# Masks added on TensorE in PSUM, batch 2's value means summed by accumulating transfers, weight splits moved off GpSimd

## Chip, cores and metric

One of the eight cores of one Trainium2 chip runs the kernel. The metric is the device time of one execution in microseconds (us); lower is better.

## What is computed

Batch 2, 8 heads, 768 tokens, head size 64, all in float32. Attention sees, for every query, the keys less than 16 positions away and 24 summaries, one for each block of 32 keys: the block's maximum of k and its mean of v. Then come two feed-forward layers over all 1536 tokens.

```python
k_sum = k.reshape(B, H, nb, 32, D).max(axis=3)
v_sum = v.reshape(B, H, nb, 32, D).mean(axis=3)
scores_l = where(|i - j| < 16, scale * q @ k.T, -1e9)
scores_s = scale * q @ k_sum.T + log(32)
a = softmax(concat([scores_l, scores_s]))
x = a @ concat([v, v_sum])
x = square(relu(x @ w_in)) @ w_out
xn = rms_norm(x) * rms_g
out = (silu(xn @ w_gate) * (xn @ w_val)) @ w_out2
```

## The kernel before

**Attention.** The 12 groups of 128 queries (6 for each batch) are worked off one after another. `scores(g)` makes two PSUM tiles of 128 x 4 x 120 scores: for each tile of 64 queries 96 keys around it and the 24 block maxima (L411). `softmax(g)` lets VectorE add a mask tile to them into SBUF (L444: -1e9 outside the window, log 32 on the summaries), takes the maxima (L448), and ScalarE takes eight exponentials with their sums (L450). `ptrans(g)` transposes the result on TensorE, and `av(g)` multiplies it with `vx`, which has four slots of 120 rows: 96 rows of v from the DMA (`vload`, L407) and 24 rows of block means. The means come from `vmean(b, c)` (L370): three loads of v (`vm_load`, L353), six float32 matmuls against the averaging matrix `ind`, and a ScalarE copy from PSUM (L387 to two slots of `vx`, L388 to `vm`); `vmput` lets GpSimd copy `vm` to the other slots (L394).

**Weights.** They arrive as 64-bit floats. `Units` takes them through a chain, one unit of 128 x 512 at a time: load (`load64`), two ScalarE instructions (`conv_a`, L176 and L177), four on VectorE (`conv_b`, L183 to L190), and `split` (L193) into a high part, rounded to the type that TensorE multiplies fastest (fp32r), and the rest. The first eight units (`wi` 0 to 3 and `wo` 0 to 3) are split on GpSimd (L197, L200), all later ones by a ScalarE cast and a VectorE subtraction.

**Feed-forward.** Every product is three fp32r matmuls, high by high, high by low and low by high (L512, L533). The first four `wi` and `wo` units run pair by pair of groups between the attention steps (`h_pair`, `y_pair`, from L699 on); the rest follows in two long loops (from L760 on).

**What sets the order.** Every engine and every DMA queue works off its own list in order. The lists are made by a planner that runs the program through a model of the chip: an instruction goes to its engine's list as soon as the model has it ready, and among those that are ready the one traced first goes first. `after(m)` puts an edge from the marked instruction to what its block traces, and only to instructions on the marked instruction's own engine; it orders issue and makes nothing wait for an end. PSUM tiles come in turn from pools of two buffers each (`psA`, tags "a" and "x" from L629 on). SyncE issues all transfers of this kernel.

Of the kernel before, what the change touches and what calls it, by code (L numbers as in the profile page):

```python
# [32 lines left out]
def tile_window_attention_moe_moe2(  # L33
# [13 lines left out]
    nc = tc.nc  # L47
# [29 lines left out]
    scale = 1.0 / math.sqrt(D)  # L77

    cpool = ctx.enter_context(tc.tile_pool(name="cpool", bufs=1))
    wpool = ctx.enter_context(tc.tile_pool(name="wpool", bufs=1))  # L80
    xpool = ctx.enter_context(tc.tile_pool(name="xpool", bufs=NCH))
    hpool = ctx.enter_context(tc.tile_pool(name="hpool", bufs=2))
# [5 lines left out]
    ident = cpool.tile([P, P], F32, name="ident")  # L88
    make_identity(nc, ident)
    um = cpool.tile([P, KW + QT], F32, name="um")  # L90
    masks = {}
    ind = cpool.tile([P, NB + P // (BLK // 2) * (NC2 - 1)], F32, name="ind")
    ss = cpool.tile([P, NG], F32, name="ss")
    rinv = cpool.tile([P, NG], F32, name="rinv")

    def constants():
        n = ind.shape[1]
        o = P // (BLK // 2) * (NC2 - 1)
        pb = BLK // 2
        nc.gpsimd.memset(ind, 1.0 / BLK)  # L100
        nc.gpsimd.affine_select(
            out=ind, in_=ind, compare_op=ALU.is_ge, fill=0.0, base=pb * o,
            pattern=[[-pb, n]], channel_multiplier=1,
        )
        nc.gpsimd.affine_select(
            out=ind, in_=ind, compare_op=ALU.is_ge, fill=0.0, base=pb - 1 - pb * o,
            pattern=[[pb, n]], channel_multiplier=-1,
        )
        nc.gpsimd.memset(um, 0.0)
        nc.gpsimd.affine_select(  # L110
            out=um, in_=um, compare_op=ALU.is_ge, fill=NEG, base=-1,
            pattern=[[1, KW + QT]], channel_multiplier=-1,
        )
        nc.gpsimd.affine_select(
            out=um, in_=um, compare_op=ALU.is_ge, fill=NEG, base=2 * WIN - 1,
            pattern=[[-1, KW + QT]], channel_multiplier=1,
        )


        mid = cpool.tile([P, NK], F32, name="mask_mid")  # L120
        nc.gpsimd.memset(mid, math.log(BLK))
        for j, n, o in ((0, G0, 0), (K1, QT, G0)):
            nc.gpsimd.tensor_copy(mid[0:QT, j : j + n], um[0:QT, o : o + n])
            nc.gpsimd.tensor_copy(mid[QT:P, j : j + n], um[QT:P, QT + o : QT + o + n])
        first = cpool.tile([P, NK], F32, name="mask_first")
        nc.gpsimd.tensor_copy(first, mid)
        nc.gpsimd.memset(first[0:QT, 0:WIN], NEG)
        last = cpool.tile([P, NK], F32, name="mask_last")
        nc.gpsimd.tensor_copy(last, mid)
        nc.gpsimd.memset(last[QT:P, NK - WIN : NK], NEG)  # L130
        masks.update(first=first, mid=mid, last=last)

# [55 lines left out]
        nc.vector.tensor_tensor(xi, xi, r, op=ALU.add)  # L190
        return x

    def split(x, nm, pool):  # L193
        w_ = wslot(f"w_{nm}")
        hi, lo = w_[:, 0], w_[:, 1]
        if pool:
            nc.gpsimd.tensor_copy(hi, x)  # L197
        else:
            nc.scalar.copy(hi, x)
        (nc.gpsimd if pool else nc.vector).tensor_tensor(lo, x, hi.bitcast(F32), op=ALU.subtract)  # L200
        return hi, lo

    class Units:
# [9 lines left out]
        def tick(self):  # L213
            n, units = self.n, self.units
            if n[3] < n[2]:
                u = units[n[3]]
                W[u] = split(self.x.pop(u), "%s%d" % u, n[3] < 2 * ROUNDS1[0])
                n[3] += 1
            if n[2] < n[1]:
                u = units[n[2]]  # L220
                with after(*((("mx", 0),) if n[2] == 0 else ())):
                    self.x[u] = conv_b(*self.a.pop(u))
                n[2] += 1
            if n[1] < n[0]:
                u = units[n[1]]
                self.a[u] = conv_a(self.raw.pop(u), "%s%d" % u)
                n[1] += 1
            self.load(min(n[2] + self.ahead, len(units), self.used + self.cap))
# [117 lines left out]
    def prep_kend(b, eng, w0, w1):  # L346
# [3 lines left out]
            state[b].unsqueeze(2).to_broadcast([P, NPAIR, w1 - w0, NB]),  # L350
        )

    def vm_load(b, c):  # L353
        state[("v", b, c)] = raw_chunk(v, b, c, f"vr{b}_{c}")

# [14 lines left out]
    def vmean(b, c):  # L370

        if c == 0:
            state["vmps"] = psA(f"vmean{b}", [K1, DM])
        ps = state["vmps"][G0:K1]
        pb = BLK // 2
        nb2 = P // pb
        vr = state.pop(("v", b, c))
        for e in range(2):
            nc.tensor.matmul(  # L379
                ps, ind[:, nb2 * (NC2 - 1 - c) : nb2 * (NC2 - 1 - c) + NB], vr[:, :, e, :],  # L380
                start=(c == 0 and e == 0), stop=(c == NC2 - 1 and e == 1),
            )
        if c == NC2 - 1:
            vm = ap_.tile([K1, DM], F32, tag="vm", name=f"vm{b}", bufs=1)[G0:K1]
            state["vm"] = vm
            if b == 0:
                nc.scalar.copy(vrows(0, 2), ps.unsqueeze(1).to_broadcast([NB, 2, DM]))  # L387
            nc.scalar.copy(vm, ps)  # L388

    def vrows(i0, n):  # L390
# [20 lines left out]
    def scores(g):  # L411
        b, r = divmod(g, GPB)
        qT = state[("qT", g)][:, :, (r % 2) * P : (r % 2 + 1) * P]
        sl = [psA(f"s{e}_{g}", [P, NPAIR, NK]) for e in range(2)]
        for p in range(NPAIR):
            for x in range(2):
                for e in range(2):
# [4 lines left out]
                        sl[e][QT * u : QT * u + QT, p, :],  # L422
                        qT[rr, p, QT * u : QT * u + QT],
                        kT[rr, p, o : o + NK],
                        start=True, stop=True,
                    )
        state[("s", g)] = sl

    def softmax(g):
# [10 lines left out]
        for i in range(parts):  # L440
            hs = slice(n * i, n * i + n)
            tv, m_, s_ = t[:, hs], mx[:, hs], sm[:, hs]
            for e in range(2 // parts * i, 2 // parts * (i + 1)):
                nc.vector.tensor_tensor(  # L444
                    te[:, e], sl[e], mk.unsqueeze(1).to_broadcast([P, NPAIR, NK]), op=ALU.add
                )
            if EXPACT(g):
                mark[("mx", g)] = nc.vector.reduce_max(m_, tv, axis=AX.X, negate=True)  # L448
                for h in range(hs.start, hs.stop):
                    mark[("exp", g)] = nc.scalar.activation(  # L450
                        t[:, h], t[:, h], AF.Exp, bias=mx[:, h : h + 1], accum_out=sm[:, h : h + 1]
                    )
            else:
                nc.vector.reduce_max(m_, tv, axis=AX.X)
# [148 lines left out]
        prep_load(0, c)  # L603
    qload(0)
    units1.load(1)
    for c in range(NC2):
        vm_load(0, c)
    vload(0)
    vload(1)
    qload(2)  # L610
    for j in (0, LK - WIN):
        nc.gpsimd.memset(kT[:, :, j : j + WIN], 0.0)
    nc.gpsimd.memset(vx[0:WIN, 0], 0.0)
# [7 lines left out]
    scores(0)  # L621
    softmax(0)
    scores(1)
    for c in range(NC2):
        vmean(0, c)
    vmput(2, 2)
    units1.load(8)
    softmax(1)
    rot["tags"] = ("a", "x")  # L629
    qprep(2)  # L630
    ptrans(0)
    group(2)
    av(0)
    vload(2)
    ptrans(1)
# [63 lines left out]
    for k_ in range(NK2):  # L699
# [10 lines left out]
        if not last:  # L710
            av(g)
        if g == GPB - 1:
            for c in range(NC2):
                vmean(1, c)
            vmput(0, 2)
        if g + 2 < NG:
            group(g + 2)
            if k_ == 0:
                for c in range(NC2):
                    prep_load(1, c)  # L720
            if g + 2 == GPB + 1:
                vmput(2, 2)
        y_pair(k_, 0)
# [2 lines left out]
        if k_ == 0:  # L726
# [1 line left out]
            prep_k(1, 0)  # L728
            y_pair(k_, 2, (lambda: prep_k(1, 1), lambda: prep_k(1, 2)))
            prep_kend(1, nc.gpsimd, 0, NW1)  # L730
            for c in range(NC2):
                vm_load(1, c)
        else:
            if g + 3 < NG:
                qprep(g + 3)
# [125 lines left out]
```

## Time and profile before

| | us |
|---|---|
| median of 3 runs | 668.17 (667.84 to 668.64) |
| the profiled execution's own time | 667.06 |
| its span, first to last instruction | 665.4 |

All rows below come from the one profiled execution. Its busy shares: TensorE 96%, VectorE 61%, ScalarE 46%, GpSimd 4%. A group's row gives the line, the engine, the operation, the tile written and those read, the shapes and the count, then the busy time in us and the mean of one in ns, then the engine's idle time just before. L12 is line 12 of the kernel printed above; SPq is SyncE's transfer queue; PEld is the load of a stationary operand, which runs beside other matmuls.

### The profile page before, as it was taken

The numbers are of one execution on the slowest core, as the hardware profiler recorded it, in microseconds if no ns is written. First come the engines' busy times: TensorE is split into PE (matmuls) and PEld (weight loads), VectorE is DVE, ScalarE is ACT, GpSimd is POOL, SyncE is SP. The second block draws the span as 40 slices with busy tenths as digits, with TensorE's granted clock in tenths as the row PEclk, the third lists the DMA queues.
The fourth block names the chain that finished last, engine by engine and source line by source line (L and its number), as shares of the span: only waits on it lengthen the run. The fifth ranks groups of instructions, "written<-read, shape, count | busy, mean of one in ns | idle before, by whom it ended". The sixth has DMA issues, their size and how long they took to land.

```text
span 665.4 us, 9357 instructions
## 1 busy us (share of the span) xinstructions
PE 642.0 (96%) x3644; PEld 530.8 (80%) x3644; DVE 402.9 (61%) x716; ACT 304.6 (46%) x656; POOL 27.3 (4%) x45
## 2 busy tenths in 40 slices
PE   7768997999999999999999999999999999999997
PEld 6566976888888888888888888888888888888885
DVE  4798777759999389528484894299613271313132
ACT  4875666557675266227253773267411231111110
POOL 3153110000000000000000000000000000000000
PEclk9878998999999999999999999999999999999999
DMA  9994644215412313101131351025300000001011
GB/s 241 290 222 112 152 136 142 75 39 179 138 64 95 96 64 96 32 1 64 32 96 32 97 162 60 1 60 161 97 0 1 0 1 0 1 1 63 1 64 64
DMA packets 76957, 53.70 MB, mean 81 GB/s; under 512 B 45040, under 2 KB 71664, under 8 KB 76912
## 3 DMA queue, kind: packets, MB, share of 16 engines
q1 hardware_dynamic: 76912, 53.09, 27.0%
q8 instruction: 29, 0.48, 0.3%
q14 instruction: 16, 0.13, 0.1%
HBM read 49.94 MB, written 3.15 MB: 80 GB/s over the span
## 4 chain that ended last, share of the span: by engine, by line
PE 87%; DVE 5%; SPq 3%; ACT 2%; issue 1%; DMA 1%; DVEq 0%; ACTq 0%
PE y L533 19%; PE h L512 18%; PE v L512 15%; PE g L512 15%; PE z L533 15%; ACT t L450 2%; PE xps L491 2%; PE pps L470 1%; SPq L308 1%; PE s L421 1%; SPq L407 1%; PE vmean L379 1%; PE xps L503 1%; PE qps L366 1%; DMA qr<-in_q_dram 1%
## 5 line engine op out<-in xcount | busy, mean ns | idle before, releaser
L512 PE MATMUL h<-xhi,w_wi 128*128 128x512 f32 (+1 forms) x480 | 134.2, 352 | 1.3 <-ACT xhi L481 1.3
L533 PE MATMUL y<-w_wo,hhi 128*128 128x512 f32 x384 | 119.0, 394 | 0.1
L807 DVE TENSOR_TENSOR sg<-v,sg 128x512 f32<-128x512 f32 x36 | 24.9, 691 | 131.2 <-PE v L512 131.2
L512 PEld LDWEIGHTS h<-xhi,w_wi 128*128 128x128 f32 x480 | 86.3, 192 | 13.3 <-ACT xhi L481 1.5
L512 PE MATMUL v<-xhi,w_wv 128*128 128x512 f32 x288 | 94.8, 390 | 0.0
L512 PE MATMUL g<-xhi,w_wg 128*128 128x512 f32 x288 | 94.5, 390 | 0.0
L533 PE MATMUL z<-w_wp,hhiz 128*128 128x512 f32 x288 | 88.0, 389 | 0.0
L512 PE MATMUL h<-xlo,w_wi 128*128 128x512 f32 (+1 forms) x240 | 84.4, 352 | 3.0 <-DVE xlo L482 3.0
L533 PEld LDWEIGHTS y<-w_wo,hhi 128*128 128x128 f32 x384 | 71.5, 189 | 14.8 <-ACT hhi L523 0.4
L533 PE MATMUL y<-w_wo,hlo 128*128 128x512 f32 x192 | 74.2, 394 | 0.2 <-DVE hlo L524 0.2
L805 ACT ACTIVATE sg<-g 128x512 f32<-128x512 f32 x36 | 21.5, 597 | 102.1 <-PE g L512 99.9
L512 PEld LDWEIGHTS v<-xhi,w_wv 128*128 128x128 f32 x288 | 54.1, 188 | 11.2
L512 PEld LDWEIGHTS g<-xhi,w_wg 128*128 128x128 f32 x288 | 54.0, 188 | 11.2
L533 PEld LDWEIGHTS z<-w_wp,hhiz 128*128 128x128 f32 x288 | 54.0, 188 | 11.1
L660 ACT ACTIVATE r<-h 128x512 f32<-128x512 f32 x48 | 28.6, 596 | 67.5 <-PE h L512 67.4
L512 PE MATMUL v<-xlo,w_wv 128*128 128x512 f32 x144 | 56.1, 389 | 0.0
L512 PE MATMUL g<-xlo,w_wg 128*128 128x512 f32 x144 | 56.0, 389 | 0.0
L533 PE MATMUL z<-w_wp,hloz 128*128 128x512 f32 x144 | 55.4, 389 | 0.0
L523 ACT CAST hhiz<-sg 128x512 fp32r<-128x512 f32 x36 | 22.3, 620 | 68.6 <-DVE sg L807 68.3
L512 PEld LDWEIGHTS h<-xlo,w_wi 128*128 128x128 f32 x240 | 46.2, 192 | 8.8 <-DVE xlo L482 3.2
L661 DVE TENSOR_TENSOR r<-h,r 128x512 f32<-128x512 f32 x48 | 32.9, 685 | 32.4 <-ACT r L660 32.4
L533 PEld LDWEIGHTS y<-w_wo,hlo 128*128 128x128 f32 x192 | 36.0, 189 | 8.1 <-DVE hlo L524 0.6
(133 smaller groups left out, 918.7 us busy)
## 6 DMA issues: line engine op xcount, KB each, us to landing
raw_wi<-in_moe_w_in_dram SPq DMA_DIRECT2D x16, 512.0 KB, 4.9
raw_wo<-in_moe_w_out_dram SPq DMA_DIRECT2D x16, 512.0 KB, 4.3
raw_wg<-in_moe_w_gate_dram SPq DMA_DIRECT2D x12, 512.0 KB, 3.5
raw_wv<-in_moe_w_val_dram SPq DMA_DIRECT2D x12, 512.0 KB, 3.6
raw_wp<-in_moe_w_out_dram SPq DMA_DIRECT2D x12, 512.0 KB, 3.5
kr<-in_k_dram SPq DMA_DIRECT2D x12, 256.0 KB, 4.2
qr<-in_q_dram SPq DMA_DIRECT2D x12, 256.0 KB, 3.9
vr<-in_v_dram SPq DMA_DIRECT2D x6, 512.0 KB, 4.9
```

Source lines behind the costliest of these rows:

```text
L308: nc.sync.dma_start(t[:, j].rearrange("p (h d) -> p h d", h=H), src[b, :, o : o + P, :].rearrange("h p d -> p h d"),)
L366: nc.tensor.transpose(ps[:, p, :], qr[:, j, p * P : (p + 1) * P], ident)
L379: nc.tensor.matmul(ps, ind[:, nb2 * (NC2 - 1 - c) : nb2 * (NC2 - 1 - c) + NB], vr[:, :, e, :], start=(c == 0 and e == 0), stop=(c == NC2 - ...
L450: mark[("exp", g)] = nc.scalar.activation(t[:, h], t[:, h], AF.Exp, bias=mx[:, h : h + 1], accum_out=sm[:, h : h + 1])
L491: nc.tensor.matmul(ps[QT * e : QT * e + QT, o : o + QT], vx[:, (2 * g + u) % NVX, 2 * p + e, :], pT[:, e * NPAIR + p, QT * u : QT * u + QT ...
L512: nc.tensor.matmul(ps, a_, b_, start=(i == 0), stop=(i == tot - 1))
L523: nc.scalar.copy(hi[:, 0:n], s[:, 0:n])
L533: nc.tensor.matmul(y, a_[:, ms], b_, start=(first and i == 0), stop=(last and i == 2))
L660: nc.scalar.activation(t, ps, AF.Relu)
L661: nc.vector.tensor_tensor(t, ps, t, op=ALU.mult)
L805: nc.scalar.activation(t, psg, AF.Silu)
L807: nc.vector.tensor_tensor(t, psv, t, op=ALU.mult)
```

## The change

Groups 0 to 3 get their masks on TensorE: ahead of a score tile's matmuls, one fp32r matmul of the identity with the mask's rounded part, and behind them one with the mask's rest, all accumulating in PSUM. The maxima and exponentials then read PSUM. `split` runs on ScalarE and VectorE for all units. The queries of groups 2 and 3 and a second weight unit are loaded ahead of v, and the means of batch 1 are queued behind the scores of group 2; one of their two copies goes from ScalarE to VectorE. For batch 2, the three loads of v and six matmuls become eight transfers issued from GpSimd, 96 x 512 floats each, of which the last seven add into the first one's tile, and a single matmul over 96 partitions.

```diff
@@ -77,6 +77,7 @@
     scale = 1.0 / math.sqrt(D)
 
     cpool = ctx.enter_context(tc.tile_pool(name="cpool", bufs=1))
+    cpool.tile([P, 0], F32, name="left")
     wpool = ctx.enter_context(tc.tile_pool(name="wpool", bufs=1))
     xpool = ctx.enter_context(tc.tile_pool(name="xpool", bufs=NCH))
     hpool = ctx.enter_context(tc.tile_pool(name="hpool", bufs=2))
@@ -88,8 +89,16 @@
     ident = cpool.tile([P, P], F32, name="ident")
     make_identity(nc, ident)
     um = cpool.tile([P, KW + QT], F32, name="um")
-    masks = {}
+    masks, mhi = {}, {}
+    NPE = 4
+    identr = cpool.tile([P, P], F32R, name="identr")
+    mlo = cpool.tile([P, NK], F32R, name="mlo")
+    for nm in ("first", "mid"):
+        mhi[nm] = cpool.tile([P, NK], F32R, name=f"mhi_{nm}")
     ind = cpool.tile([P, NB + P // (BLK // 2) * (NC2 - 1)], F32, name="ind")
+    NE = 8
+    PV = S // NE
+    indv = cpool.tile([PV, NB], F32, name="indv")
     ss = cpool.tile([P, NG], F32, name="ss")
     rinv = cpool.tile([P, NG], F32, name="rinv")
 
@@ -105,6 +114,16 @@
         nc.gpsimd.affine_select(
             out=ind, in_=ind, compare_op=ALU.is_ge, fill=0.0, base=pb - 1 - pb * o,
             pattern=[[pb, n]], channel_multiplier=-1,
+        )
+        pv = BLK // NE
+        nc.gpsimd.memset(indv, 1.0 / BLK)
...
         nc.gpsimd.memset(um, 0.0)
         nc.gpsimd.affine_select(
@@ -129,6 +148,12 @@
         nc.gpsimd.tensor_copy(last, mid)
         nc.gpsimd.memset(last[QT:P, NK - WIN : NK], NEG)
         masks.update(first=first, mid=mid, last=last)
+        nc.gpsimd.tensor_copy(identr, ident)
+        nc.gpsimd.tensor_copy(mhi["first"], first)
+        nc.gpsimd.tensor_copy(mhi["mid"], mid)
+        nc.gpsimd.tensor_tensor(
+            mlo, mid, mhi["mid"].bitcast(F32), op=ALU.subtract
+        )
 
 
 
@@ -190,14 +215,11 @@
         nc.vector.tensor_tensor(xi, xi, r, op=ALU.add)
         return x
 
-    def split(x, nm, pool):
+    def split(x, nm):
         w_ = wslot(f"w_{nm}")
         hi, lo = w_[:, 0], w_[:, 1]
-        if pool:
-            nc.gpsimd.tensor_copy(hi, x)
-        else:
-            nc.scalar.copy(hi, x)
-        (nc.gpsimd if pool else nc.vector).tensor_tensor(lo, x, hi.bitcast(F32), op=ALU.subtract)
+        nc.scalar.copy(hi, x)
+        nc.vector.tensor_tensor(lo, x, hi.bitcast(F32), op=ALU.subtract)
         return hi, lo
 
     class Units:
@@ -214,7 +236,7 @@
             n, units = self.n, self.units
             if n[3] < n[2]:
                 u = units[n[3]]
-                W[u] = split(self.x.pop(u), "%s%d" % u, n[3] < 2 * ROUNDS1[0])
+                W[u] = split(self.x.pop(u), "%s%d" % u)
                 n[3] += 1
             if n[2] < n[1]:
                 u = units[n[2]]
@@ -350,6 +372,22 @@
             state[b].unsqueeze(2).to_broadcast([P, NPAIR, w1 - w0, NB]),
         )
 
+    vsum = xpool.tile([P, KD, CH], F32R, tag="xhi", name="vsum")
+    vsum = vsum[0:PV, 0].bitcast(F32).rearrange("p (h d) -> p h d", h=H)
+
+    def vs_load(b):
+        src = v[b].rearrange("h (p e) d -> p h e d", e=NE)
+        nc.gpsimd.dma_start(vsum, src[:, :, 0, :])
+        for e in range(1, NE):
+            nc.gpsimd.dma_start(vsum, src[:, :, e, :], accum_op=ALU.add)
+
+    def vs_mean(b):
+        ps = psA(f"vmean{b}", [K1, DM])[G0:K1]
+        nc.tensor.matmul(ps, indv, vsum.rearrange("p h d -> p (h d)"), start=True, stop=True)
+        vm = ap_.tile([K1, DM], F32, tag="vm", name=f"vm{b}", bufs=1)[G0:K1]
+        state["vm"] = vm
+        nc.scalar.copy(vm, ps)
+
     def vm_load(b, c):
         state[("v", b, c)] = raw_chunk(v, b, c, f"vr{b}_{c}")
 
@@ -384,7 +422,7 @@
             vm = ap_.tile([K1, DM], F32, tag="vm", name=f"vm{b}", bufs=1)[G0:K1]
             state["vm"] = vm
             if b == 0:
-                nc.scalar.copy(vrows(0, 2), ps.unsqueeze(1).to_broadcast([NB, 2, DM]))
+                nc.vector.tensor_copy(vrows(0, 2), ps.unsqueeze(1).to_broadcast([NB, 2, DM]))
             nc.scalar.copy(vm, ps)
 
     def vrows(i0, n):
@@ -412,6 +450,11 @@
         b, r = divmod(g, GPB)
         qT = state[("qT", g)][:, :, (r % 2) * P : (r % 2 + 1) * P]
         sl = [psA(f"s{e}_{g}", [P, NPAIR, NK]) for e in range(2)]
+        wide = [P, NPAIR, NK]
+        if g < NPE:
+            for s_ in sl:
+                mh = mhi["mid" if r else "first"]
+                nc.tensor.matmul(s_, identr, mh.unsqueeze(1).to_broadcast(wide), start=True, stop=False)
         for p in range(NPAIR):
             for x in range(2):
                 for e in range(2):
@@ -422,8 +465,13 @@
                         sl[e][QT * u : QT * u + QT, p, :],
                         qT[rr, p, QT * u : QT * u + QT],
                         kT[rr, p, o : o + NK],
-                        start=True, stop=True,
+                        start=g >= NPE, stop=g >= NPE,
                     )
+        if g < NPE:
+            for s_ in sl:
+                mark[("s", g)] = nc.tensor.matmul(
+                    s_, identr, mlo.unsqueeze(1).to_broadcast(wide), start=False, stop=True
+                )
         state[("s", g)] = sl
 
     def softmax(g):
@@ -440,15 +488,23 @@
         for i in range(parts):
             hs = slice(n * i, n * i + n)
             tv, m_, s_ = t[:, hs], mx[:, hs], sm[:, hs]
-            for e in range(2 // parts * i, 2 // parts * (i + 1)):
+            for e in range(2 // parts * i, 2 // parts * (i + 1)) if g >= NPE else ():
                 nc.vector.tensor_tensor(
                     te[:, e], sl[e], mk.unsqueeze(1).to_broadcast([P, NPAIR, NK]), op=ALU.add
                 )
             if EXPACT(g):
-                mark[("mx", g)] = nc.vector.reduce_max(m_, tv, axis=AX.X, negate=True)
+                src = [t[:, h] for h in range(H)]
+                if g < NPE:
+                    src = [s_[:, p] for s_ in sl for p in range(NPAIR)]
+                    for e in range(2 // parts * i, 2 // parts * (i + 1)):
+                        mark[("mx", g)] = nc.vector.reduce_max(
+                            mx[:, NPAIR * e : NPAIR * (e + 1)], sl[e], axis=AX.X, negate=True
+                        )
+                else:
+                    mark[("mx", g)] = nc.vector.reduce_max(m_, tv, axis=AX.X, negate=True)
                 for h in range(hs.start, hs.stop):
                     mark[("exp", g)] = nc.scalar.activation(
-                        t[:, h], t[:, h], AF.Exp, bias=mx[:, h : h + 1], accum_out=sm[:, h : h + 1]
+                        t[:, h], src[h], AF.Exp, bias=mx[:, h : h + 1], accum_out=sm[:, h : h + 1]
                     )
             else:
                 nc.vector.reduce_max(m_, tv, axis=AX.X)
@@ -603,11 +659,12 @@
         prep_load(0, c)
     qload(0)
     units1.load(1)
+    qload(2)
+    units1.load(2)
     for c in range(NC2):
         vm_load(0, c)
     vload(0)
     vload(1)
-    qload(2)
     for j in (0, LK - WIN):
         nc.gpsimd.memset(kT[:, :, j : j + WIN], 0.0)
     nc.gpsimd.memset(vx[0:WIN, 0], 0.0)
@@ -621,15 +678,16 @@
     scores(0)
     softmax(0)
     scores(1)
-    for c in range(NC2):
-        vmean(0, c)
-    vmput(2, 2)
+    softmax(1)
     units1.load(8)
-    softmax(1)
+    qprep(2)
     rot["tags"] = ("a", "x")
-    qprep(2)
     ptrans(0)
     group(2)
+    with after(("s", 2)):
+        for c in range(NC2):
+            vmean(0, c)
+    vmput(2, 2)
     av(0)
     vload(2)
     ptrans(1)
@@ -710,14 +768,15 @@
         if not last:
             av(g)
         if g == GPB - 1:
-            for c in range(NC2):
-                vmean(1, c)
+            vs_mean(1)
             vmput(0, 2)
         if g + 2 < NG:
             group(g + 2)
             if k_ == 0:
                 for c in range(NC2):
                     prep_load(1, c)
+                with after(("s", 4)):
+                    vs_load(1)
             if g + 2 == GPB + 1:
                 vmput(2, 2)
         y_pair(k_, 0)
@@ -728,8 +787,6 @@
             prep_k(1, 0)
             y_pair(k_, 2, (lambda: prep_k(1, 1), lambda: prep_k(1, 2)))
             prep_kend(1, nc.gpsimd, 0, NW1)
-            for c in range(NC2):
-                vm_load(1, c)
         else:
             if g + 3 < NG:
                 qprep(g + 3)
```

## Rows read from the trace of the kernel before

**Rows 1.** The page's head: the span and TensorE's busy time.

```profile
span 665.4 us, 9357 instructions
...
PE 642.0 (96%) x3644; PEld 530.8 (80%) x3644; DVE 402.9 (61%) x716; ACT 304.6 (46%) x656; POOL 27.3 (4%) x45
```

**Rows 2.** Busy time by engine in stretches: length, busy us (instructions), granted clock, DMA.

```profile
12.00:28.48 16.48, 12.26 (x113) 6.94 (x111) 10.85 (x25) 12.54 (x44) 3.54 (x4) 0.90 0.96 266
28.48:57.21 28.73, 20.60 (x261) 18.00 (x262) 28.73 (x49) 20.76 (x59) 12.17 (x11) 0.88 0.86 233
...
89.24:112.66 23.42, 19.52 (x219) 16.91 (x219) 18.01 (x34) 20.86 (x70) 2.02 (x2) 1.00 0.51 158
```

**Rows 3.** Chain that ended last, in order of time: start us, us, what.

```profile
20.16 3.56 DMA qr<-in_q_dram
...
30.28 0.65 DVE t L444
...
56.55 0.65 PE pps L470 x4
...
83.95 5.27 PE vmean L379 x12
...
179.60 2.72 PE y L533 x12
```

**Rows 4.** Groups by line and shape, VectorE, 0 to 70 us.

```profile
L444 DVE TENSOR_TENSOR t<-s,mask_mid 128x480 f32<-128x480 f32 x8 | 5.2, 646 | 1.6 <-PE s L421 1.6
...
L184 DVE TENSOR_SCALAR x_wo<-x_wo 128x512 uint32<-128x512 uint32 x4 | 3.7, 934 | 0.0
L183 DVE TENSOR_SCALAR x_wo<-x_wo 128x512 f32<-128x512 f32 x4 | 3.1, 780 | 0.0
...
L458 DVE TENSOR_SCALAR sm<-sm 128x4 f32<-128x4 f32 x6 | 2.7, 458 | 1.8 <-ACT t L450 1.8
...
L482 DVE TENSOR_TENSOR xlo<-xps,xhi 128x512 fp32r<-128x512 f32 x4 | 2.7, 676 | 0.0
...
L184 DVE TENSOR_SCALAR x_wi<-x_wi 128x512 uint32<-128x512 uint32 x4 | 1.7, 433 | 0.0
```

**Rows 5.** Timeline, 34 to 52 us: start us, us, engine, line.

```profile
34.72 1.15 PE L491 MATMUL xps<-pT,vx 120*64 120x64 f32 x32 [1.38 <-POOL w_wi L197]
...
38.75 0.16 DVE L458 TENSOR_SCALAR sm<-sm 128x4 f32<-128x4 f32 x1
...
47.06 2.10 POOL L200 TENSOR_TENSOR w_wo<-x_wo,w_wo 128x512 fp32r<-128x512 f32 x1
...
47.92 1.52 DVE L184 TENSOR_SCALAR x_wo<-x_wo 128x512 uint32<-128x512 uint32 x1
...
50.86 1.05 PE L421 MATMUL s<-kT,qT 64*64 64x120 f32 x32
```

**Rows 6.** Timeline of ScalarE at the two copies of means, idle time in brackets.

```profile
20.95 1.00 ACT L387 COPY vx<-vmean 24x1024 f32<-24x1024 f32 x1 [2.03 <-PE vmean L379]
...
89.24 0.58 ACT L388 COPY vm<-vmean 24x512 f32<-24x512 f32 x1 [4.67 <-PE vmean L379]
```

**Rows 7.** Groups by line and shape, ScalarE, 0 to 70 us.

```profile
L523 ACT CAST hhi<-r 128x512 fp32r<-128x512 f32 x2 | 1.2, 620 | 2.7 <-DVE r L661 2.7
```

**Rows 8.** Timeline of SyncE's transfer queue.

```profile
41.82 5.92 SPq L308 DMA_DIRECT2D kr<-in_k_dram  x6
50.49 2.26 SPq L407 DMA_DIRECT2D vx<-in_v_dram  x4
```

**Rows 9.** Transfers: size, median us from issue to landing; then vr's shortest, median, longest.

```profile
kr<-in_k_dram SPq DMA_DIRECT2D x12, 256.0 KB, 4.2
...
vx<-in_v_dram SPq DMA_DIRECT2D x22, 64.0 KB, 2.7
...
DMA to landing us min/median/max: 3.8/4.9/8.0
```

**Rows 10.** Timeline of GpSimd, 10 to 170 us.

```profile
22.56 1.03 POOL L394 COPY vx<-vm 24x1024 f32<-24x1024 f32 x1 [3.28 <-ACT vm L388]
```

More of the change, by code (lines that the diff above doesn't have):

```diff
@@ L107, in constants @@
             pattern=[[pb, n]], channel_multiplier=-1,
+        )
+        pv = BLK // NE
+        nc.gpsimd.memset(indv, 1.0 / BLK)
+        nc.gpsimd.affine_select(
+            out=indv, in_=indv, compare_op=ALU.is_ge, fill=0.0, base=0,
+            pattern=[[-pv, NB]], channel_multiplier=1,
+        )
+        nc.gpsimd.affine_select(
+            out=indv, in_=indv, compare_op=ALU.is_ge, fill=0.0, base=pv - 1,
+            pattern=[[pv, NB]], channel_multiplier=-1,
         )
@@ L447, in softmax @@
             if EXPACT(g):
-                mark[("mx", g)] = nc.vector.reduce_max(m_, tv, axis=AX.X, negate=True)
+                src = [t[:, h] for h in range(H)]
[4 more added lines that the diff above has]
+                            mx[:, NPAIR * e : NPAIR * (e + 1)], sl[e], axis=AX.X, negate=True
+                        )
+                else:
+                    mark[("mx", g)] = nc.vector.reduce_max(m_, tv, axis=AX.X, negate=True)
                 for h in range(hs.start, hs.stop):
                     mark[("exp", g)] = nc.scalar.activation(
-                        t[:, h], t[:, h], AF.Exp, bias=mx[:, h : h + 1], accum_out=sm[:, h : h + 1]
+                        t[:, h], src[h], AF.Exp, bias=mx[:, h : h + 1], accum_out=sm[:, h : h + 1]
                     )
```

## The prediction

> **What bounds it now.** I read the page first: TensorE is busy for 642.0 of 665.4 us [rows 1], so 23 us at most can go without taking work from TensorE. The busy time by stretch says where they are: from 12 to 57.21 us TensorE is busy for 12.26 + 20.60 = 32.9 of 45.2 us, from 89.24 to 112.66 for 19.52 of 23.42 [rows 2]. Everything else is nearly full.
>
> Who holds the first stretch? Up to 28.48 us nobody does: VectorE works 10.85 of 16.48 us, ScalarE 12.54, and the chain passes through the load of the second query tile, 3.56 us [rows 2, 3]. From 28.48 us VectorE is busy without a break, 28.73 of 28.73, and the chain lies on it from 30.28 to 56.55 [rows 2, 3]. So the early stage is bound by VectorE, behind a late start.
>
> The later gap begins with batch 2's means: twelve passes of a float32 matmul hold TensorE for 5.27 us [rows 3], ScalarE's list stands still for 4.67 us until they end [rows 6], and then ScalarE works 20.86 of 23.42 us [rows 2], a gap after a gap.
>
> **The change part by part, as a sum.**
>
> *Means of batch 2.* Six matmuls become one: two passes for twelve at 0.44 us each (5.27 / 12), so 0.88 for 5.27, **-4.4 us** of TensorE. ScalarE stood still for as long and is the busiest engine after it, so I carry this over whole.
>
> *VectorE's stretched instructions.* With GpSimd at work on a split (2.10 us at 47.06) VectorE's shift took 1.52 us at 47.92 [rows 5], where the same form takes 0.43 [rows 4]. Summed by groups, against 0.43, 0.43 and 0.16 us: four L184 cost 2.0 us too much, four L183 1.4, six L458 1.7 [rows 4, 5], 5.1 in all. Without the splits on GpSimd these go.
>
> *Masks and splits.* VectorE loses eight adds of 0.65 (5.2) and gets eight subtractions of 0.68 (5.4) [rows 4] and one copy of means, which took ScalarE 1.00 [rows 6]. ScalarE gets eight casts of 0.62 [rows 7], 5.0, and loses that copy. The maxima and exponentials read PSUM at about the old price, I assume; no row has that form.
>
> *The early stage.* VectorE goes from 10.85 + 28.73 = 39.6 to 39.6 - 5.1 - 5.2 + 5.4 + 1.0 = 35.7 us; ScalarE from 12.54 + 20.76 = 33.3 to 33.3 + 5.0 - 1.0 = 37.3. ScalarE becomes the busier of the two. The 45.2 us held 45.2 - 39.6 = 5.6 in which VectorE waited. The query tile's 3.56 of these should go, as it is issued behind the first weight unit, some 10 us earlier. That leaves 37.3 + 5.6 - 3.6 = 39.3 us, a gain of 5.9. But ScalarE would then be busy for 95% of the stage, and where it was busiest it reached 20.86 / 23.42 = 89% [rows 2]; at 89% the stage takes 41.9 and the gain is 3.3. I take **-4.5 us**. The ends: 0, if ScalarE's new casts cost what VectorE gains; 3.9 + 5.6 = 9.5, if VectorE stays the bound and every wait goes.
>
> *Masks on TensorE.* Sixteen matmuls of 480 columns at 2.72 / 12 x 480 / 512 = 0.21 us [rows 3] are 3.4 us, and double that where the granted clock, 0.88 to 0.90 on the mean here [rows 2], is at 1.2 instead of 2.4 GHz. 12.3 us of TensorE are free there: **0**. Without that cover they would cost 3.4 to 6.8.
>
> *Means of batch 1 behind group 2.* The same 5.27 us, moved from idle time to a stage that still has some; but now a copy on VectorE and the GpSimd copy of 1.03 [rows 10] stand between them and `av(0)`. What is late next is `av(1)`, at 34.72 [rows 5]. With group 2's scores at about 20 instead of 27 us the means are there by 20 + 5.3 + 1.6 + 1.0 = 28, before it: **0**. Held back longer, score tiles occupy two of four PSUM buffers until their exponentials end; that lies beside ScalarE's work, already counted.
>
> *Queues.* SyncE issues the same transfers in another order, v about 2 us later, and three fewer afterwards: 0.
>
> *The eight transfers.* GpSimd issues them, and each waits for the one before. The block that is to hold them behind group 4's scores orders only TensorE, the marked instruction's engine, so it doesn't hold them. The planner pulls ahead what is ready: batch 2's k was issued at 41.82, before the v of group 4 at 50.49, which is traced earlier [rows 8]. So I expect the first at 5 to 10 us. No row shows an adding transfer, and one is 96 x 512 x 4 bytes, 197 KB. Loads of 256 KB land 4.2 us after issue, those of 64 KB after 2.7, the slowest v load after 8.0 [rows 9]. Eight in a row take 22 to 64 us; I take 4.2, the row nearest in size, so 34. They end at 40 to 45 us, far ahead of the 79 where the means are now needed: hidden. Their 1.5 MB move into a stage whose transfer engines are 86 to 96% busy at 233 to 266 GB/s [rows 2]; if all of it delayed the weights it would cost 6 us. I take **0**, as VectorE and not a load is what the chain waits for there.
>
> One page weighs on this. By the Trainium skill's page "DMA: Bandwidth & Descriptors", section "Anatomy of one DMA — SWDGE (gpsimd) path", such a transfer takes 2.0 us and its bytes at 436 GB/s: by an estimate from it 2.5 us each, 20 in all, and the sum would stay as it is.
>
> Sum: -4.4 - 4.5 = **-8.9 us**. Against the profiled execution's 667.06 that is 658.2; the median of the runs is 1.1 above that execution, so I predict **659.3 us**, in a range of its own of 654 to 664. A difference under 0.2% (1.3 us) can't be told from none.
>
> **Rivals.**
>
> *Slower: GpSimd's list blocks `av(1)`.* The copy of means to slots 2 and 3 of `vx` stands in GpSimd's list among eight transfers that each wait for the last. `av(1)` should want it by 34.7 - 4.5 = 30 us [rows 5]. Put behind six transfers, it runs at 5 + 6 x 4.2 = 30 us, just in time [rows 9]. If a transfer takes 5.8 us the copy comes at 40, 10 us late, and the gain of 8.9 is gone; this is the point. At 8.0 it comes at 53, 23 us late, and the time is 682. Between, at 7 us, 675. For it: the planner's list is fixed by modelled durations; the transfers run beside the busiest loads; VectorE and GpSimd stretch each other [rows 5]. Against: one transfer is smaller than the loads that take 4.2 us. 21%.
>
> A rule speaks for this rival. The Trainium skill's page "SBUF — State Buffer", section "SBUF: two separate sides", says that a transfer issued from GpSimd stalls while VectorE holds the port that both share, as GpSimd can't write its descriptors. The trace shows a lock of the kind only for GpSimd's arithmetic [rows 5].
>
> *ScalarE eats the early gain.* The casts in ScalarE's list wait for VectorE's results and hold the exponentials behind them. Then only the -4.4 is left: 663.8. For: 37.3 us of work on an engine that waited often. Against: the exponentials of group 1 no longer stand behind 2.03 us of waiting for the means [rows 6]. 13%.
>
> *No change: the transfers do wait for group 4's scores.* Those came at 50.86 us [rows 5]; 46 after the gain. Eight of 4.2 end at 80, where the means are needed at 79, and nothing is lost; at 5.3 each they end at 88 and the 8.9 are given back: 668. For: it is what the code seems to mean. Against: the rule on engines. 6%.
>
> **How the numbers follow.** The forecast has 60%. Faster: forecast and ScalarE's case, 0.73. Same: 0.06. Slower: 0.21. The range of 652 to 672 takes in the forecast's ends, ScalarE's case, no change and the nearer part of the slow rival; outside lie most of that rival and a better overlap than I count on.
>
> **What would show it.** Right: one `vmean` matmul pair of 0.9 us before 80; ScalarE's idle time before the copy to `vm` gone; L183, L184 and L458 at their short durations; scores of group 2 near 20 us; ScalarE over 85% busy until the y chain starts at about 52. Wrong: `av(1)` or a `vx` copy waiting for a transfer on GpSimd; the vsum transfers after 46 us; over 5.8 us for each; TensorE waiting for a mask that GpSimd made late; a stage of 20 to 50 us in which ScalarE's casts wait for VectorE.

## The result, and the profile after

The changed kernel takes **676.08 us** (median of 4, 674.4 to 678.6) against 668.40 on the same chip: a ratio of **1.0145, 95% interval 1.0115 to 1.0176**. It is 1.5% slower where the forecast was 1.3% faster, and it lies above the range's 672. The profiled execution took 677.55 us.

The page's head, the counterpart of [rows 1]:

```profile
span 675.6 us, 9371 instructions
...
PE 654.4 (97%) x3650; PEld 539.5 (80%) x3650; DVE 398.8 (59%) x718; ACT 306.4 (45%) x663; POOL 21.5 (3%) x44
```

VectorE and GpSimd work less, as planned. TensorE's busy time rose by 12.4 us, though some 4 us of passes were taken out and some 5 put in. The stretches of [rows 2], columns as there:

```profile
12.00:28.48 16.48, 13.42 (x127) 8.57 (x126) 11.13 (x27) 14.40 (x60) 0.00 (x0) 0.77 1.02 278
28.48:57.21 28.73, 24.09 (x200) 16.54 (x202) 22.30 (x44) 17.82 (x44) 5.91 (x5) 0.72 0.96 216
89.24:112.66 23.42, 19.11 (x112) 14.58 (x111) 12.11 (x19) 12.42 (x44) 4.62 (x4) 0.79 0.54 94
```

TensorE looks busier than before in the first two, but its granted clock fell from 0.90, 0.88 and 1.00 to 0.77, 0.72 and 0.79, and in the last stretch it got through less: 112 matmul records, of mixed sizes, where 219 were. VectorE and ScalarE are far from full. So read on by what TensorE waits for. The chain of waits (start us, us, what), the counterpart of [rows 3]:

```profile
20.48 1.32 PE s L464 x16
...
26.24 7.75 PE vmean L417 x12
...
61.77 2.07 PE y L589 x9
...
79.71 1.42 POOL kT L370
81.12 4.54 DMA vsum<-in_v_dram
...
85.94 7.17 DMA vsum<-in_v_dram
...
93.40 5.74 DMA vsum<-in_v_dram
...
99.43 4.41 DMA vsum<-in_v_dram
...
103.88 1.90 PE vmean L386 x2
...
107.58 5.42 PE y L589 x12
```

Two places stand out. At 26.24 us batch 1's means run alone. From 79.71 to 103.84 the chain is one engine's list, GpSimd's (timeline; in brackets the idle time before and what ended it), the counterpart of [rows 10]:

```profile
35.98 1.03 POOL L432 COPY vx<-vm 24x1024 f32<-24x1024 f32 x1 [24.05 <-ACT vm L426]
36.97 0.96 POOL L380 DMA_DIRECT2D vsum<-in_v_dram  x1
41.78 1.32 POOL L382 DMA_DIRECT2D vsum<-in_v_dram  x1 [3.85 <-DMA vsum<-in_v_dram]
48.69 1.33 POOL L382 DMA_DIRECT2D vsum<-in_v_dram  x1 [5.59 <-DMA vsum<-in_v_dram]
53.64 1.31 POOL L382 DMA_DIRECT2D vsum<-in_v_dram  x1 [3.62 <-DMA vsum<-in_v_dram]
79.71 1.47 POOL L370 COPY kT<-ksum 128x1152 f32<-128x1152 f32 x1 [24.76 <-DVE ksum L356]
81.12 1.55 POOL L382 DMA_DIRECT2D vsum<-in_v_dram  x1
```

Four transfers go out, then a copy for batch 2's `kT` (`prep_kend`, an old instruction of GpSimd's) waits 24.76 us for VectorE's block maxima, and four transfers stand behind it although nothing they need is missing. The last lands at 103.84; TensorE had nothing to do from 100.6 on. What that does to its clock shows in stretches of 4 us (length, TensorE's busy us, granted clock, DMA):

```profile
100.00:104.00 4.00, 0.71 (x4) 0.86 0.56 49
104.00:108.00 4.00, 4.00 (x19) 0.50 0.02 4
108.00:112.00 4.00, 4.00 (x11) 0.50 0.00 0
```

After 3.3 us without work it runs at 1.2 instead of 2.4 GHz for some 10 us, at the price of 5 more. The same happens early, at the place that the means have left:

```profile
16.00:20.00 4.00, 0.94 (x10) 1.00 1.12 339
20.00:24.00 4.00, 4.00 (x30) 0.62 0.94 226
24.00:28.00 4.00, 4.00 (x20) 0.50 0.98 264
```

In the kernel before, the twelve passes ran there, from 14.9 us on, and TensorE was busy for 3.46 of the 4 us from 16 to 20. Now they come behind group 2 at the low clock, in 7.75 us, ahead of `av(0)` and everything after it. VectorE stands idle for them, and ScalarE behind VectorE's copy, the counterpart of [rows 6]:

```profile
34.02 1.22 DVE L425 COPY vx<-vmean 24x1024 f32<-24x1024 f32 x1 [6.48 <-PE vmean L417]
```

```profile
35.27 0.58 ACT L426 COPY vm<-vmean 24x512 f32<-24x512 f32 x1 [6.82 <-DVE vx L425]
```

**A book-keeping for what follows.** From each profiled execution I add up, in steps of 2 us, TensorE's idle time and its busy time multiplied by (1 - granted clock), which is what the low clock costs. "Last y" is the start of the last `y` matmul fed by a high part, which closes the first layer; behind it before and after take 300.1 and 300.4 us to the end of the span, so it carries the whole difference.

| kernel | ratio, 95% interval | idle + low clock, 0 to 60 us | 80 to 140 us | last y |
|---|---|---|---|---|
| before | 1 | 15.1 + 4.6 | 4.0 + 1.5 | 365.3 |
| changed | 1.0145 (1.0115 to 1.0176) | 9.7 + 10.7 | 6.5 + 6.3 | 375.2 |
| changed, once more | 1.0152 (1.0122 to 1.0182) | 11.7 + 10.5 | 7.0 + 4.9 | 375.2 |
| means of batch 1 early | 1.0010 (0.9986 to 1.0035) | 9.3 + 6.3 | 4.8 + 0.0 | 364.7 |
| means of batch 2 by loads | 1.0019 (1.0001 to 1.0037) | 9.9 + 9.6 | 2.7 + 0.0 | 366.3 |
| kT copy on VectorE | 1.0011 (0.9989 to 1.0033) | 9.9 + 10.5 | 3.1 + 1.7 | 366.5 |
| early + loads | 0.9987 (0.9965 to 1.0008) | 7.6 + 6.6 | 2.3 + 1.7 | 363.8 |
| early + kT on VectorE | 0.9987 (0.9964 to 1.0011) | 7.6 + 5.0 | 2.7 + 6.8 | 364.1 |
| fill of the late wait, 4 | 1.0091 (1.0054 to 1.0127) | 11.5 + 10.4 | 3.6 + 1.7 | 371.9 |
| v first | **0.9932** (0.9903 to 0.9960) | 9.2 + 5.1 | 2.6 + 0.0 | 361.6 |
| v first, masks on VectorE | **0.9913** (0.9879 to 0.9946) | 12.4 + 9.8 | 0.3 + 0.0 | 360.9 |

A profiled execution lies up to 2.2 us off its kernel's median, so differences of 1 or 2 us between the last three columns carry nothing.

### The profile page after: what moved, and what is told of

Its sections match the earlier page's. It is cut to its first block, busy times and chain, and to the rows that moved or that the text cites. A ratio compares the mean times of both kernels' runs of the same rounds, so it can differ in the third digit from the quotient of the medians.

```text
span 675.6 us, 9371 instructions
## 1 busy us (share of the span) xinstructions
PE 654.4 (97%) x3650; PEld 539.5 (80%) x3650; DVE 398.8 (59%) x718; ACT 306.4 (45%) x663; POOL 21.5 (3%) x44
## 4 chain that ended last, share of the span: by engine, by line
PE 89%; DMA 4%; DVE 4%; SPq 1%; ACT 1%; issue 0%; POOL 0%; DVEq 0%; POOLq 0%; ACTq 0%
PE h L568 19%; PE y L589 19%; PE v L568 15%; PE g L568 15%; PE z L589 14%; DMA vsum<-in_v_dram 3%; PE s L464 2%; PE xps L547 1%; PE pps L526 1%; PE vmean L417 1%; SPq L330 1%; PE xps L559 1%; DMA qr<-in_q_dram 1%; DVE t L516 1%; PE qps L404 1%; DVE mx L500 0%
```

## The experiments

### Undoing one part

**Batch 1's means early again.** In the changed kernel:

```diff
+    for c in range(NC2):
+        vmean(0, c)
+    vmput(2, 2)
+    units1.load(8)
     softmax(1)
-    units1.load(8)
...
-    with after(("s", 2)):
-        for c in range(NC2):
-            vmean(0, c)
-    vmput(2, 2)
     av(0)
```

> The changed kernel with batch 1's means and their copy back in front of softmax(1), as before; all else as changed. Theory (the 12 passes of vmean(0) behind group 2 hold TensorE's list at 26.2 us for 7.75 us, VectorE idle 6.5 and ScalarE idle 6.8 behind it, and y starts 4.6 us late): the first y pass comes back to about 57 us and the time falls by 4 to 6.5 us from 676.1, to 670 to 672. Rival (the early stage is late because of the masks on TensorE and the splits moved to ScalarE and VectorE): the passes wait where they now stand as well, y stays at 61 to 62 us, and the time within 1.5 us of 676.

Measured: 667.13 us, `y` from 56.7. The gain of 9 us (1.0145 to 1.0010) is twice what I gave the early stage. The kT copy came earlier too, at 75.84, and the last transfer landed 4.7 us earlier; the wait shrank to 1.9 us, and the clock held:

```profile
L386 PE MATMUL vmean<-vsum,indv 96*24 96x512 f32 x2 | 1.0, 601 | 1.9 <-DMA vsum<-in_v_dram 1.9
```

**Batch 2's means by loads.** `vs_mean(1)` becomes the three `vmean(1, c)`, `vm_load(1, c)` returns behind `prep_kend`, `vs_load` goes.

> The changed kernel with batch 2's means by three loads and 12 passes, as before, and no accumulating transfers. Theory (GpSimd's list, with batch 2's kT copy standing between transfers 4 and 5 until 79.7 us, ends the eight at 104 us and delays vs_mean and av by some 5.6 us net of the ten passes saved): time falls by 4 to 7 us, to 669 to 672, and the first y pass stays at 61 to 62 us. Rival (the second loss of some 5 us is the clock of 0.79 in 89 to 113 us or the later start of everything, and the transfers are paid by the passes saved): the ten passes come back, and the time rises to 678 to 681.

Measured: 668.45, `y` at 60.6 still. The whole loss went, a little more than I gave it, although ten passes came back; the rival is out. GpSimd still makes the kT copy in this run, so it is not the copy by itself that costs.

**kT copy on VectorE.**

```diff
-            prep_kend(1, nc.gpsimd, 0, NW1)
+            prep_kend(1, nc.vector, 0, NW1)
```

> The changed kernel with batch 2's kT copy on VectorE, so that nothing stands between the eight transfers on GpSimd. Theory: transfers 5 to 8 follow at 58 to 73 us and the last lands by about 78 us, before vs_mean is wanted; the time falls by what the transfers cost plus what the saved passes give, 5.6 + 4.4 = up to 10 us, to 666 to 669. Rival (the transfers themselves are too slow in a chain or collide with other traffic): the last lands after 90 us all the same and the time stays over 673.

Measured: 668.57. One word of the code brings back 9 us, with the early stage as late as ever (`y` at 61.5). Transfers five to eight follow at 58 to 75 us (GpSimd's list, then the two passes in the chain):

```profile
58.44 1.31 POOL L382 DMA_DIRECT2D vsum<-in_v_dram  x1 [3.32 <-DMA vsum<-in_v_dram]
...
75.15 1.31 POOL L382 DMA_DIRECT2D vsum<-in_v_dram  x1 [3.27 <-DMA vsum<-in_v_dram]
...
98.75 0.97 PE vmean L386 x2
```

TensorE doesn't wait for them, and its loss in 80 to 140 us falls from 12.8 to 4.8. This is the cleanest of the three: **the loss came through the order of GpSimd's list.** The time can't be told from before's (0.9989 to 1.0033), so the ten passes saved still don't show.

**Both means undone.**

> Both undone: batch 1's means in front of softmax(1) and batch 2's means by loads and passes; masks on TensorE, no splits on GpSimd, query tile and weight load ahead of v stay. Theory: the two losses add (4 to 6.5 and 4 to 7), so 664 to 667, under the 668.2 of the kernel before by what the early stage gained. Rival (the parts that stay cost something too): 668 or over.

Measured: 665.65. Right in size; but the two losses don't add: each run alone had brought back nearly everything, since both end in the one wait at 104 us. Where nothing waits for the transfers, the late means cost little: 1.0011 against 0.9987 with the kT copy on VectorE, which can't be told apart, and 1.0019 against 0.9987 with loads.

### One part at a time

**The last run with the masks on VectorE** (`NPE = 0`).

> The run with both means undone (batch 1's in front of softmax(1), batch 2's by loads and passes), and the masks back on VectorE as well; no splits on GpSimd, query tile and weight load ahead of v stay. Theory (with the masks on TensorE the exponentials read the scores out of PSUM, so the PSUM tiles come free only behind ScalarE: in the run with both undone the mask pass of scores(3) waits 3.1 us for ScalarE and scores(3) ends at 41.7 us where the kernel before has it at 33.3): scores(3) comes at 32 to 36 us, the first y pass at 51 to 53 us in place of 54.8, and the time falls to 661 to 664. Rival (VectorE bounds the stretch to 57 us, and the eight mask adds of 0.65 us are what the masks on TensorE save): y at 57 to 60 us and the time 668 to 671.

Measured: 666.29, ratio 1.0000 (0.9982 to 1.0018); `y` only from 65.1. Neither came true: against the run with both undone (0.9987) what the masks on TensorE are worth can't be told from nothing. They do hold PSUM, as TensorE's timeline of the run with both undone shows at scores(3):

```profile
35.14 0.48 PE L457 MATMUL s<-mhi_mid,identr 128*128 128x480 f32 x1 [3.08 <-ACT t L506]
```

Why taking them off TensorE doesn't shorten the time is not shown.

**Means early, and kT copy on VectorE**, all else as changed.

> The changed kernel with batch 1's means in front of softmax(1) and batch 2's kT copy on VectorE; all else as changed, the eight accumulating transfers with nothing between them included. Theory (ten passes of 0.44 us saved, transfers hidden): 4.4 us under the run with both undone, so 661 to 662. Rival (TensorE waits in 84 to 113 us anyway, so that passes saved there become waits for VectorE and ScalarE): 664 to 667, with TensorE busy less in that stretch than in the run with both undone.

Measured: 666.26, the rival's range: the ten passes saved show nothing against the run with both undone (665.65). The early loss fell to 12.6 us, but in this execution the clock was low from 106 to 119 us behind a wait of 2.07 us for ScalarE.

**Masks on TensorE alone**, put into the kernel before.

> The kernel before with the masks of groups 0 to 3 added on TensorE, and nothing else of the change that issues instructions in the loops. Theory (PSUM tiles held until the exponentials are done give back what VectorE saves): 667 to 670, VectorE's busy time in 12 to 57 us down by some 5 us and its idle time up by as much. Rival (VectorE bounds this stretch, so its 5.2 us come off): 662 to 664.

Measured: 665.53, 0.9985 (0.9969 to 1.0001), between the two ranges. VectorE's work from 12 to 57 us fell from 39.37 to 36.52, TensorE's busy time rose from 32.66 to 36.99. A shift between engines, no gain that can be told from none.

**Transfers alone**, put into the kernel before, with the kT copy on VectorE. Splits stay on GpSimd.

> The kernel before with batch 2's means from eight accumulating transfers and batch 2's kT copy on VectorE, so that only splits stand around the transfers on GpSimd. Theory (a stall of TensorE for the transfers is what costs, the passes saved give little): last transfer lands before 95 us, no stall of TensorE, time 664 to 668. Rival 1 (ten passes of 0.44 us come off the path): 661 to 663. Rival 2 (the transfers cost in themselves, wherever they stand): over 670.

Measured: 668.79, 1.0033 (1.0011 to 1.0055), over the theory's range. The splits now stand between the transfers: the second goes out at 42.12 us and the third at 61.51. But the means' two passes run at 97.48 without a wait, so that is not shown to be the cause of the 0.3%.

### Filling TensorE's idle time

Work that changes no result, put where TensorE waits, tells a wait from the clock behind it.

**Late fill.** In `vs_mean`, ahead of its matmul (first 8, then 4 times):

```diff
+        t6 = state[("t", GPB)][:, 0:4].rearrange("q h n -> q (h n)")
+        for _ in range(8):
+            nc.tensor.matmul(ps[:, 0 : 4 * NK], ident[:, 0:NB], t6, start=True, stop=True)
```

> The changed kernel with eight passes of 480 columns more on TensorE, just ahead of group 7's scores and of the two passes that sum batch 2's means; they read group 6's softmax and write the PSUM tile that the two passes then overwrite, so the output is the same. In the changed kernel TensorE stands idle for 3.3 us there, until the last transfer lands at 103.9 us, and its granted clock is 0.50 from 102.6 to 113 us. Theory (it is the low clock behind the wait, more than the wait, that costs): the clock stays at 1.00 in 102 to 113 us, and the time falls by 3 to 6 us, to 670 to 673, although work is added. Rival (the wait alone costs, the clock falls for other reasons): no less than 676, up to 3.5 us more.

Measured: 675.7, no gain. Each instruction became two passes, so the fill ran for 6.6 us, twice the wait; but the clock stayed at 1.00 from 84 to 144 us. With 4:

> As the run that fills TensorE's wait for the last transfer, with half the fill: four instructions in place of eight, which that run showed as two passes of 0.41 us each, so 3.3 us in place of 6.6, the length of the wait itself. Theory (the low clock of 10 us behind the wait costs as much as the wait): TensorE at 1.00 in 102 to 116 us, no wait over 1 us for the transfer, and the time 3 us under the longer fill, 671 to 673: faster than the changed kernel although work is added. Rival (the wait alone is what costs): 675 or over.

Measured: 673.8, ratio 1.0091 (1.0054 to 1.0127): 0.54% less than the changed kernel, just over the range given, and the intervals meet only at 1.012. With 3.3 us of work *added*, the last `y` came 3.3 us earlier. The stretches shown above, in this run:

```profile
100.00:104.00 4.00, 4.00 (x26) 1.00 0.54 48
104.00:108.00 4.00, 4.00 (x20) 1.00 0.03 5
108.00:112.00 4.00, 4.00 (x23) 1.00 0.08 17
```

So, as far as intervals that meet at their ends can show it, the low clock behind the wait was a real part of the loss, and the wait the other.

**Early fill.** Behind `scores(1)`, in a block `after(("s", 1))`, idle matmuls of 128 columns into the tile `ws` (28, then 8).

> The changed kernel with 28 idle passes of 128 columns more on TensorE behind group 1's scores, at about 16 us, where the kernel before ran batch 1's 12 means and the changed kernel leaves TensorE idle for 3.1 of 4 us (granted clock 0.50 from 21 to 31 us behind it); the output is the same. Theory (the means at their old place were work in free time that kept the clock up): 1.00 in 20 to 31 us, the 12 passes behind group 2 take 5.3 us in place of 7.75, the first y pass comes 3 to 5 us earlier than 61.8 us, and the time falls by 3 us or more (to 673 or less; to 667 if the transfers then end ahead of their wait as with the means in their old place). Rival (it is the place of the means in TensorE's list that costs, not the clock): y within 1.5 us of 61.8, time 675 to 678.

Measured: 666.24, 10 us less, with the clock at 1.00 and the means in 5.27 us:

```profile
15.92 6.25 PE ws L683 x56
...
25.10 0.42 PE s L472
25.52 0.21 PE s L457
...
27.12 5.27 PE vmean L417 x12
```

`y` was no earlier (63.6), though, and the planner had moved the first transfer up to 12.4 us and left three behind the kT copy in place of four. The run mixes two causes. With 8:

> As the run that fills TensorE's idle time at 16 us, with 8 instructions (16 passes, about 1.8 us) in place of 28 (6.3 us); four of the eight transfers stay behind batch 2's kT copy on GpSimd, as in the changed kernel. Theory (idle TensorE at 16 to 20 us brings the low clock at 21 to 31 us, and with it the lateness of everything behind): granted clock over 0.80 in 20 to 30 us, the 12 passes in 5.3 to 6 us, first y pass at 57 to 59 us, time 667 to 672. Rival (the longer fill helped only because the transfers went ahead and fewer were left behind the kT copy): the last transfer lands after 100 us, time over 674.

Measured: 673.78, between the two. TensorE still idled, for 1.56 of the 4 us from 20 to 24, and ran at 0.51 behind that; the last transfer landed at 104.6. Four transfers stood behind the kT copy here and three with the longer fill, where that copy also came 4 us sooner (76.34 against 80.36). That points to the transfers' place for much of the longer fill's gain, but the early loss differs too (17.2 us here, 13.5 there), so what the early low clock costs by itself stays open.

**The changed kernel once more.**

> The changed kernel once more, beside the others on one chip: 1.012 to 1.018 of the kernel before. Theory: a wait of 2 us or more for the last transfer near 100 to 104 us and the clock at 0.50 behind it in this execution too. Rival (the low clock after the wait was of that one execution): the clock at 1.00 in 104 to 113 us with the time no lower.

Measured: 676.63, ratio 1.0152. The wait was 3.4 us; the clock was 0.89 and 0.68 in the two stretches from 104 on, less low than before, and fell again to 0.52 at 124. The last `y` is at 375.2 in both.

### A version that beats both

**v first.** The changed kernel with means early, the query tile and the weight load behind v as before, the PSUM pools rotated ahead of `qprep(2)` as before, and the kT copy on VectorE. The load order's part of the edit:

```diff
-    qload(2)
-    units1.load(2)
     for c in range(NC2):
         vm_load(0, c)
     vload(0)
     vload(1)
+    qload(2)
```

> The changed kernel with batch 1's means in front of softmax(1), the query tile and the weight load behind v again, and batch 2's kT copy on VectorE; masks on TensorE, no splits on GpSimd and the accumulating transfers stay. Theory (what pays of the change is the masks on TensorE; the means belong in TensorE's free time at 15 to 20 us, which needs v's loads first; the transfers cost nothing when none of them is waited for): 663 to 665, the lowest yet. Rival (every part is worth nothing because TensorE has work enough to the end): 665.5 to 667.

Measured: **661.83 us, 0.9932 (0.9903 to 0.9960)**, better than expected. v lands in time, the twelve passes run from 15.2 us, the transfers go out from 24.57 to 72.11, and the late stretch loses 2.6 us. Against the run that differs only in the order of these loads and in the PSUM pools of `qprep(2)` (means early, kT on VectorE: 0.9987) these two are worth 0.5% together. Then the same without the transfers and with the kT copy on GpSimd again; and with the transfers, but the masks on VectorE (the `after` block around the transfers, which orders only TensorE's list, goes too):

> The version that beats both (661.8), with batch 2's means by loads and 12 passes in place of the accumulating transfers, and batch 2's kT copy on GpSimd again. Theory (ten passes saved are TensorE's own time, and they pay where none of the transfers is waited for): 4.3 us more, 665 to 667. Rival (the transfers are worth nothing there either; the gain is in the rest): 661 to 663.

> The version that beats both (661.8), with the masks of groups 0 to 3 added on VectorE. Theory (the 16 mask passes take some 5 us of TensorE and give back about as much of its idle time): 661 to 664. Rival (masks on TensorE are what pays): 665 to 668.

Measured: 669.29 (1.0033, 1.0009 to 1.0057) and **661.39** (0.9913, 0.9879 to 0.9946). The first lies outside both ranges given. The transfers and the kT copy's place are worth 7 us together here; the masks on TensorE can't be told from nothing. And the load order has no worth of its own: without the transfers the same edit goes the other way, from 0.9987 (both means undone) to 1.0033.

The kernels with v first and the means early also answer what the splits do. Ratios to the kernel before:

| | splits on GpSimd | splits on ScalarE and VectorE, one copy of means on VectorE |
|---|---|---|
| means of batch 2 by loads | 1; with masks on TensorE 0.9985 | 1.0033, with masks on TensorE |
| by transfers, kT copy on VectorE | 1.0033 | **0.9913**; with masks on TensorE **0.9932** |

Each of the two edits loses 0.3 to 0.5% alone, and together they gain 0.7 to 0.9%. That fits a list that holds either splits or transfers well and not both; but as the transfers between the splits were not waited for, the mechanism is argued and not shown.

## Why the prediction was wrong

**The eight transfers: 0 was the term that failed.** I expected the first "at 5 to 10 us" as the planner pulls ahead what is ready, and the last "at 40 to 45 us". The first went out at 36.97: it stands behind `vmput`'s copy, which waited for the moved means. I had priced a transfer by the load nearest in size, 4.2 us; it landed 4.6 after issue in the median and 7.2 at most, and the next followed 4.8 to 7.5 us later, 5.8 on the mean where nothing stood between. The estimate of 2.5 us from the Trainium skill's page "DMA: Bandwidth & Descriptors", section "Anatomy of one DMA — SWDGE (gpsimd) path", was further off. Price was not what decided: with the kT copy on VectorE eight of them, from 36.74 on, had all gone out by 75.15. What decided is a row of GpSimd's list in the kernel before that the prediction doesn't count:

```profile
75.20 2.00 POOL L348 COPY kT<-ksum 128x1152 f32<-128x1152 f32 x1 [13.74 <-DVE ksum L334]
```

It waits for VectorE until 75.20. I had counted the queue's own new work and `vmput`, and never this copy of `kT`. So four transfers stood behind it, the last landed at 103.84 and not by 45, and in place of 0 the term cost a wait of 3.3 us and about 5 us of low clock; moving the one copy gave 9 us back.

**The slow rival** named the right engine's list, the right kind of block and, by luck, a range (675 to 682) that holds the result. Its turning price of 5.8 us is what a step of the chain took on the mean, but its place was wrong: not `vmput` behind transfers at 30 us, but transfers behind `prep_kend` at 80. The case of no change is out too: four transfers had gone out by 53.64 us, ahead of group 4's scores at 57.02.

**Means of batch 2, -4.4.** The passes fell as said, 5.27 us to 0.97 at the full clock. But here they came at 103.88, behind a wait of 3.3 us and with the clock at 0.50 (1.90 us). Without that wait the gain still didn't show in two pairs (668.57 against 668.45, 666.26 against 665.65); with v first the two passes are part of the 7 us. No run has the passes alone.

**Means of batch 1 behind group 2: 0 failed too.** "The means are there by 28": they were there at 34.0. I had asked which instruction would want them (`av(1)`); on an engine's in-order list the question is what stands behind them. `av(0)`, the next transpose and scores(3) did, and VectorE's and ScalarE's lists as well. I had also counted the old place as idle time that costs nothing to give up. It was work that kept TensorE going between two softmaxes. Most of what this cost came through the kT copy, which ran 4.5 us later than before (79.71 against 75.20).

**The early stage, -4.5.** Group 2's scores came at 20.48, the wait for the query tile went, and the stretched instructions too: the shifts that took 0.93 us [rows 4] take 0.42. Yet `y` starts at 61.6 instead of 52.8. ScalarE did not become the bound: in the 45.2 us to 57.21 it worked 32.2 us and not 37.3, with VectorE at 33.4. Summing an engine's work found the slack but not who waits for whom. Nor is the first `y` a measure of the time: it starts at 53.2 in the run with the transfers alone (1.0033), at 65.1 in the one with the masks on VectorE and both means undone (1.0000), and at 59.1 in the fastest.

**Masks on TensorE, 0.** They cost 0.63 us a pair at the full clock, as the lines of the early fill show (0.42 + 0.21), 5.0 us for eight pairs and not 3.4. 0 was right in sum (0.9985 alone), and by the cover that I named: in that run TensorE's busy time from 12 to 57 us rose by 4.3 us, out of 12.3 that were idle. (fp32r is the faster of the two types that this kernel multiplies: 0.23 us for 512 columns, against two passes of 0.44 for float32. No run has a third.)

**What the book-keeping says.** Between the changed kernel and the one with the kT copy on VectorE, TensorE's loss in 80 to 140 us differs by 12.8 - 4.8 = 8.0 us, and the last `y` by 8.7. The early loss did not differ from before (20.4 to 19.7): the saving of 5.4 us of idle time went back in 6.1 us of low clock.

Not settled: how much the early low clock costs by itself, why the order of v, query tile and weight pays with the transfers and costs without them, why splits and transfers lose alone and gain together, and why one chained transfer follows the last after 4.3 us (kT copy on VectorE) and another after 8.55 (v first).

## What to carry to other kernels

Before new work goes onto a quiet engine's queue, list everything already on that queue and when each entry's input is ready; a chain of dependent transfers should not be split by an instruction that waits for a late result. On a kernel whose TensorE is 96% busy, cost an edit in TensorE's time: passes, plus waits, plus what the low clock takes behind a wait. Work in an idle gap is not free to move away, as it may be what keeps the clock up, and one wait that several edits feed makes each of them look like the whole loss when undone alone. Two edits can also lose alone and gain together, as the splits and the transfers do here: try them in both combinations before one is dropped.

## What was not expected of the hardware

An idle gap of 3.3 us cost about 8: behind it TensorE's granted clock was 0.50 for some 10 us of full work. The section "What's actually happening" of the Trainium skill's page "TensorE: Matmul & The Clock Gate" says that the low clock is the default and that activity releases it; the trace agrees that idle time brings it (0.71 us busy of 4, then 0.50), and the filled run that steady work keeps it at 1.00. The gap's length alone did not fix the price: a gap of 3.4 us in the second execution left 0.89 and 0.68.

An adding transfer of 192 KB took 4.2 to 7.2 us from issue to landing, and in a chain one followed the last after 5.8 us on the mean. Whether it slowed what ran beside it no run isolates: the two fastest versions have the chain unbroken, but so has the changed kernel with the kT copy on VectorE (1.0011).
